# RetNet attention and MLP on one core: v's first chunks loaded as float32 by SyncE, and a reordered start

## The chip, the cores and the metric

The kernel runs on one core of one Trainium2 chip. The metric is the device time of one execution in microseconds. Before the change it is 302.19 us, the median of 3 runs (302.04 to 302.5).

## What is computed

The reference is a retention layer (attention with a decay mask instead of a softmax) followed by a two-layer MLP:

```python
B, H, S, D = 8, 8, 576, 64            # q, k, v: float32 [B, H, S, D]
scores = (1/sqrt(D)) * q @ k.transpose(0, 1, 3, 2)
gamma = 1 - 2.0 ** (-5 - arange(H))   # one decay for each head
Dmat = where(i >= j, gamma ** (i - j), 0)
ret = (scores * Dmat) @ v
x = ret.transpose(0, 2, 1, 3).reshape(B*S, H*D)   # 4608 x 512
h = x @ w_in                          # 512 x 2048
out = (h * sigmoid(1.702 * h)) @ w_out            # 2048 x 512, float32 out
```

## The kernel before

The decay gamma^(i-j) is split: v's rows are scaled by a factor of their position j (`vfac`, made from exponentials in `vraw`), and the result by a factor of i (`gq`). What is left of Dmat is a 0/1 mask. The sequence of a batch goes in chunks of 128 tokens (five, the last of 64); a running state (`psZ`, copied to `zq`) carries the earlier chunks. Batch 0 is done this way, chunk by chunk; batches 1 to 7 are done in wider steps woven into the matmuls of the MLP, which take nearly all of TensorE's time.

A recorder (`Rec.op`) notes every operation with the keys that it reads and writes, and derives the semaphore waits; each engine then runs its operations in the order in which they were noted. So the order of the calls in the code is the order of each engine's queue.

All loads go through GpSimd's queue (`load`, L216; the recorder's `POOL`) and are cast from float32 to bfloat16 on the way. A load of one chunk of q, k or v for all 8 heads has 1024 rows of 256 B. `load_w_in` (L240) and `load_w_out` (L245) load the MLP's weights on the same queue.

Batch 0's start, where the change lies, is a software pipeline over chunks n = 0 to 3:

- `transposes(n)` (L373): TensorE turns q and k of the chunk into one PSUM bank (`psT`, key "W").
- `evac_t(n)` (L379): ScalarE copies them to `qk`.
- `scores(n)` (L392) on TensorE into `psS`, then `mask_s(n)` (L402) on VectorE to `sm`; together `intra(n)`. There is one `psS`, so scores n+1 wait for mask n.
- `values(n)` (L415, L427, L442): TensorE's matmuls of `sm` and v, the state and the state's part; `evac_z` (L467) on ScalarE copies the state, `evac_o` (L480) on VectorE multiplies by `gq` and writes `xT`, the MLP's input.
- `scale_v(n)` (L358) multiplies a chunk of v by `vfac`; chunk 0's runs on VectorE, those of 1 to 3 on GpSimd between weight loads (chunk 3's into a second buffer `v3`, L362).
- `fill(count)` (L807): matmuls on zeros (`idle`) that keep TensorE busy where it would wait; they write `psH[0]`.

`constants_first` makes positions by two iotas on GpSimd (`posj`, `posa`), from them the identity, the mask and positions on VectorE (`rel`, `ident`, `mask`, `posi`), and on ScalarE eight exponentials for `vraw` (L273) and four for `gq`. `later_gq` (L327) makes the rest of `gq`. `constants_mask3` (L349) folds v's factor of chunk 3 into a mask.

After the four chunks, `hidden_split` (L712) begins the MLP with units f = 0 and 1, `hidden` (L695) goes on with f = 2 to 15 (f = 2, 3 use w_in's second load, f = 4 to 7 its third), and `project` (L746) multiplies by w_out. The third load of w_in covers columns of f = 4 to 7, the fourth those of f = 8 to 11.

The buffer `gT[1]` holds activations of the MLP's odd row blocks; at the start it is free, and `mask3` and `v3` lie in its rows 8 to 13.

## Time and profile before

| | |
|---|---|
| median of 3 runs | 302.19 us |
| the profiled execution | 302.22 us |
| its span, first to last instruction | 300.42 us |
| TensorE matmul busy | 292.5 us (97%) |
| VectorE busy | 122.3 us (41%) |
| ScalarE busy | 127.9 us (43%) |
| GpSimd busy | 154.8 us (52%) |
| DMA queue of GpSimd | 118384 packets, 18.36 MB |
| DMA queue of SyncE | 36432 packets, 16.92 MB |
| first w_in matmul starts at | 18.24 us |

The profile is one execution recorded by the hardware profiler; times in it count from the first instruction of the span, and 1.8 us of the execution lie outside it. Engines are named PE (TensorE matmul), PEld (its weight loads), DVE (VectorE), ACT (ScalarE), POOL (GpSimd) and SP (SyncE). A row names the engine, the line of the kernel, the operation and the tiles (out<-in).

### The profile page before, as it was taken

The page shows a single profiled execution, that of the slowest core. Times are in us where ns is not written, and L with a number is a line of the kernel's source. Part 1 is how long each engine was busy: PE and PEld are TensorE (multiplying, and loading weights), DVE is VectorE, ACT ScalarE, POOL GpSimd, SP SyncE. Part 2 cuts the span into 40 slices and gives each one's busy share as a digit, 9 for nine tenths or more (in the row PEclk, how much of TensorE's full clock was granted, in tenths as well). Part 3 has the DMA queues.
Part 4 walks back from the last instruction along what each step waited for, and adds up shares of the span by engine and source line. Part 5 has one row for each costly group of instructions (what it writes and reads, how often), then busy time and mean ns, then how long its engine had stood idle before and what let it go on. Part 6 is the DMA issues. An engine that isn't in the chain of part 4 may idle for free.

```text
span 300.4 us, 7696 instructions
## 1 busy us (share of the span) xinstructions
PE 292.5 (97%) x3395; PEld 148.9 (50%) x3395; DVE 122.3 (41%) x213; ACT 127.9 (43%) x215; POOL 154.8 (52%) x208
## 2 busy tenths in 40 slices
PE   7899999899999999999999999999999999999996
PEld 3454455757645444444444444544444444444444
DVE  6589735362525555334506143265236503000012
ACT  7676426614445503560375036602570266026600
POOL 8999679998967868677985796000000000000000
PEclk9999999999999999999999999999999999999999
DMA  9999999999999999999999999904720210020012
GB/s 69 145 183 207 177 171 161 193 129 138 178 143 163 163 117 191 173 136 142 135 213 138 127 186 155 85 1 101 173 41 2 105 37 2 0 107 35 0 57 85
DMA packets 154850, 35.78 MB, mean 119 GB/s; under 512 B 145472, under 2 KB 150336, under 8 KB 154816
## 3 DMA queue, kind: packets, MB, share of 16 engines
q0 software_dynamic: 118384, 18.36, 95.8%
q1 hardware_dynamic: 36432, 16.92, 31.6%
q8 instruction: 27, 0.44, 0.6%
q14 instruction: 7, 0.06, 0.1%
HBM read 36.70 MB, written 9.44 MB: 154 GB/s over the span
## 4 chain that ended last, share of the span: by engine, by line
PE 88%; POOL 4%; DMA 3%; ACT 2%; DVE 1%; issue 1%; POOLq 0%
PE psH L746 27%; PE psH L695 24%; PE psU L746 13%; PE psU L695 12%; DMA w_in_sb<-in_moe_w_in_dram 3%; PE psA L560 2%; PE psA L588 2%; PE psH L730 2%; PE psA L602 1%; PE psA L576 1%; POOL st_q L216 1%; PE psA L746 1%; POOL st_k L216 1%; PE psA L772 1%; POOL st_v L216 1%; ACT qk L379 1%
## 5 line engine op out<-in xcount | busy, mean ns | idle before, releaser
L746 PE MATMUL psH<-w_out_sb,gT 128*128 128x512 bf16 x368 | 87.0, 379 | 0.0
L695 PE MATMUL psH<-xT,w_in_sb 128*128 128x512 bf16 x332 | 79.2, 379 | 0.2 <-DMA w_in_sb<-in_moe_w_in_dram 0.2
L649 DVE TENSOR_TENSOR xT<-psA,gq 128x768 bf16<-128x768 f32 x21 | 20.1, 958 | 115.2 <-PE psA L576 115.2
L700 ACT ACTIVATE gT<-psH 128x512 bf16<-128x512 f32 x83 | 49.5, 597 | 26.0 <-PE psH L695 26.0
L229 POOL DMA_DIRECT2D st_k<-in_k_dram x70 | 53.0, 782 | 14.1 <-DMA st_k<-in_k_dram 13.1
L746 PEld LDWEIGHTS psH<-w_out_sb,gT 128*128 128x128 bf16 x368 | 35.0, 98 | 40.7 <-DVE sm L660 0.4
L229 POOL DMA_DIRECT2D st_v<-in_v_dram x70 | 52.0, 770 | 6.0 <-DMA st_v<-in_v_dram 4.0
L695 PEld LDWEIGHTS psH<-xT,w_in_sb 128*128 128x128 bf16 x332 | 32.1, 98 | 38.6 <-DMA w_in_sb<-in_moe_w_in_dram 0.7
L695 PE MATMUL psU<-xT,w_in_sb 128*128 128x512 bf16 x172 | 44.2, 379 | 0.1
L746 PE MATMUL psU<-w_out_sb,gT 128*128 128x512 bf16 x176 | 43.9, 379 | 0.0
L216 POOL DMA_DIRECT2D st_q<-in_q_dram x40 | 36.0, 899 | 9.7 <-DMA st_q<-in_q_dram 7.3
L755 ACT ACTIVATE osb<-psH 128x512 f32<-128x512 f32 x21 | 12.5, 597 | 57.6 <-PE psH L746 54.5
L700 ACT ACTIVATE gT<-psU 128x512 bf16<-128x512 f32 x43 | 25.7, 597 | 13.5 <-PE psU L695 13.5
L695 PEld LDWEIGHTS psU<-xT,w_in_sb 128*128 128x128 bf16 x172 | 16.5, 98 | 20.0 <-ACT gT L719 0.6
L746 PEld LDWEIGHTS psU<-w_out_sb,gT 128*128 128x128 bf16 x176 | 16.6, 98 | 19.4 <-issue 0.5
L358 DVE TENSOR_TENSOR st_v<-st_v,vfac 128x512 bf16<-128x512 bf16 x37 | 24.2, 683 | 0.9 <-DMA st_v<-in_v_dram 0.9
L676 DVE TENSOR_TENSOR zacc<-zacc,psA 128x256 f32<-128x256 f32 x49 | 20.5, 418 | 8.3 <-PE psA L588 7.1
L755 ACT ACTIVATE osb<-psU 128x512 f32<-128x512 f32 x10 | 6.0, 597 | 33.0 <-PE psU L746 33.0
L660 DVE TENSOR_TENSOR sm<-psA,maskw 128x768 bf16<-128x768 f32 x21 | 19.9, 948 | 0.0
L379 ACT ACTIVATE qk<-psA 128x1024 bf16<-128x1024 bf16 x10 | 10.2, 1022 | 10.5 <-PE psA L373 10.5
L758 DVE COPY osb<-psH 128x512 f32<-128x512 f32 x2 | 1.4, 692 | 26.9 <-PE psH L746 26.9
L560 PEld LDWEIGHTS psA<-sm,st_v 64*64 64x64 bf16 x504 | 7.5, 108 | 9.4 <-issue 8.7
(103 smaller groups left out, 231.0 us busy)
## 6 DMA issues: line engine op xcount, KB each, us to landing
out_dram<-osb SPq DMA_DIRECT2D x35, 256.0 KB, 4.0
st_q<-in_q_dram POOLq DMA_DIRECT2D x32, 128.0 KB, 7.2
st_k<-in_k_dram POOLq DMA_DIRECT2D x57, 64.0 KB, 7.5
st_v<-in_v_dram POOLq DMA_DIRECT2D x57, 64.0 KB, 7.3
w_out_sb<-in_moe_w_out_dram POOLq DMA_DIRECT2D x4, 512.0 KB, 11.8
w_in_sb<-in_moe_w_in_dram POOLq DMA_DIRECT2D x3, 512.0 KB, 8.9
st_k<-in_k_dram POOLq DMA_DIRECT2D x4, 128.0 KB, 4.5
st_v<-in_v_dram POOLq DMA_DIRECT2D x4, 128.0 KB, 4.6
```

The lines of the kernel that those rows point to most:

```text
L216: paced(R.op("POOL", lambda e, d=d, s=s: e.dma_start(d, s), w=[(nm, sl, c)], dma=(nm, sl, c), own=pace()))
L229: paced(R.op("POOL", lambda e: [e.dma_start(d, s) for d, s in parts], w=[(nm, sl, c)], dma=(nm, sl, c), parts=2, own=pace()))
L358: R.op(eng, lambda e: e.tensor_tensor(t, t, f, ALU.mult), r=[("vfac", min(b, 1))], w=[("v", sl, c)])
L379: R.op("ACT", lambda e: e.activation(qk[n % NQK].ap(), psT, AF.Copy), w=[("qk", n % NQK, 0), ("qk", n % NQK, 1)], ps=["W"])
L560: i = e.matmul(psA[half(t), 2 + u, at : at + 64], rows_of(st_v, m_out, g, u, 4 * u + 2 * t + j), smw[si(m_out)][half(r), j, 2 * blk + t, : ...
L649: R.op("DVE", lambda e: e.tensor_tensor(xT[:, :, t0 : t0 + 192].rearrange("p (u j) n -> p u j n", u=2), psA[:, 2:4, 0:384].rearrange("p u ...
L660: R.op("DVE", lambda e: e.tensor_tensor(o, i, k, ALU.mult), r=["maskw"], w=[("sm", si(m))], ps=["S"])
L676: R.op("DVE", lambda e, to=to, src=src, was=was: e.tensor_tensor(to, was, src, ALU.add), r=[("zacc", (blk - 1) % 3)], w=[("zacc", blk)], p ...
L695: i = e.matmul(bank, w_in_sb[:, a, 128 * f : 128 * f + 128], xT[:, a, 512 * c : 512 * c + 512], start=(a == 0), stop=(a == 3))
L700: R.op("ACT", lambda e: e.activation(gT[c % 2][:, f, :], bank, AF.Gelu_apprx_sigmoid), w=[("gT", c % 2, f)], ps=[key])
L746: i = e.matmul(bank, gT[c % 2][:, f, 128 * r : 128 * r + 128], w_out_sb[:, f, :], start=(f == 0), stop=(f == NF - 1))
L755: R.op("ACT", lambda e: e.activation(osb[m].ap(), bank, AF.Copy), w=[("osb", m)], ps=[key])
```

## The change

- `load_early(c)`: v's chunks 0 to 2 of batch 0 are loaded by SyncE as float32, without a cast, into rows 0 to 5 of `gT[1]` (two rows for each chunk), first of all. `scale_v` of these chunks reads the float32 copy and writes `st_v`.
- `scale_v(0)` and `scale_v(1)` are on VectorE ahead of the first `mask_s`; `scale_v(2)` is on GpSimd between the second and third load of w_in, `scale_v(3)` after the third.
- The first transposes alternate between two banks: chunks 1 and 3 go to `psH[0]` (`turned`), the fills to `psH[1]`.
- `transposes(1)` and `evac_t(1)` come ahead of `intra(0)`, and so on: each chunk's transposes one step earlier in TensorE's order. There are 13, 4, 3, 2 and 2 fills (24) in place of 14, 4, 3, 3 and 3 (27).
- One VectorE product (`posj` by `lnh`) and one exponential make `vraw`, in place of eight exponentials.
- The memsets (`constants_zero`) come first on VectorE; `mask` is made last of the first constants.
- GpSimd's order: q's chunk 0 ahead of the iotas, then k's chunk 0, q and k of chunks 1 to 3, w_in's first load, v's chunk 3, and the other weight loads.

```diff
@@ -158,6 +158,7 @@
         tiny = sb("tiny", [P, 1], FP32)
         idle = sb("idle", [P, 512], BF16)
         lng = sb("lng", [P, HP], FP32)
+        lnh = sb("lnh", [P, H], FP32)
         vraw = sb("vraw", [P, H, NC], FP32)
         vfac = [sb(f"vfac{i}", [P, H, NC], FP32) for i in range(2)]
         zacc = sb("zacc", [P, 3, 2 * 128], FP32)
@@ -250,35 +251,52 @@
             R.op("POOL", lambda e: e.iota(t.ap(), pattern, base=base, channel_multiplier=mul,
                                           allow_small_or_imprecise_dtypes=True), w=[name])
 
-        def constants_first():
-            iota(posj, "posj", [[128, NC]], 0, 1)
-            iota(posa, "posa", [[1, 128]], 0, 0)
-            R.op("DVE", lambda e: e.tensor_scalar(
-                rel.ap(), posa.ap(), posj[:, 0:1], None, ALU.subtract),
-                r=["posa", "posj"], w=["rel"])
+        def load_early(c):
+            s = v[0, :, 128 * c : 128 * c + 128, :].rearrange("h p d -> p h d")
+            d = early(c).rearrange("p (h d) -> p h d", d=DH)
+            R.op("SP", lambda e: e.dma_start(d, s), w=early_keys(c), dma=("early", c))
+
+        def early(c):
+            return gT[1][:, 2 * c : 2 * c + 2, :].rearrange("p f n -> p (f n)").bitcast(FP32)
+
+        def early_keys(c):
+            return [("gT", 1, 2 * c), ("gT", 1, 2 * c + 1)]
+
+        def constants_zero():
             R.op("DVE", lambda e: e.memset(idle.ap(), 0.0), w=["idle"])
+            for h in range(H):
+                R.op("DVE", lambda e, h=h: e.memset(lnh[:, h : h + 1], -math.log(gamma(h))),
+                     w=["lnh"])
             for hp in range(HP):
                 for hh in range(2):
                     R.op("DVE", lambda e, hp=hp, hh=hh: e.memset(
                         lng[64 * hh : 64 * hh + 64, hp : hp + 1],
                         math.log(gamma(2 * hp + hh))), w=[("lng", hp, hh)])
+
+        def constants_first():
+            iota(posj, "posj", [[128, NC]], 0, 1)
+            iota(posa, "posa", [[1, 128]], 0, 0)
+            R.op("DVE", lambda e: e.tensor_tensor(
+                vraw.ap(), posj.ap().unsqueeze(1).to_broadcast([P, H, NC]),
+                lnh.ap().unsqueeze(2).to_broadcast([P, H, NC]), ALU.mult),
+                r=["posj", "lnh"], w=["vraw"])
+            R.op("DVE", lambda e: e.tensor_scalar(
+                rel.ap(), posa.ap(), posj[:, 0:1], None, ALU.subtract),
+                r=["posa", "posj"], w=["rel"])
             R.op("DVE", lambda e: e.tensor_single_scalar(ident.ap(), rel.ap(), 0.0, ALU.is_equal),
                  r=["rel"], w=["ident"])
-            R.op("DVE", lambda e: e.tensor_single_scalar(mask.ap(), rel.ap(), 0.0, ALU.is_ge),
-                 r=["rel"], w=["mask"])
             for c in range(1, NC):
                 R.op("DVE", lambda e, c=c: e.tensor_single_scalar(
                     posi[:, c - 1, :], posa.ap(), 128.0 * c, ALU.add), r=["posa"], w=["posi"])
-            for h in range(H):
-                R.op("ACT", lambda e, h=h: e.activation(
-                    vraw[:, h, :], posj.ap(), AF.Exp, scale=-math.log(gamma(h))),
-                    r=["posj"], w=["vraw"])
+            R.op("ACT", lambda e: e.activation(vraw.ap(), vraw.ap(), AF.Exp), w=["vraw"])
             for hp in range(HP):
                 R.op("ACT", lambda e, hp=hp: e.activation(
                     gq[:, hp, 0:128], posa.ap(), AF.Exp, scale=lng[:, hp : hp + 1]),
                     r=["posa", ("lng", hp, 0), ("lng", hp, 1)], w=[("gq", 0)])
             R.op("DVE", lambda e: e.tensor_single_scalar(
                 vfac[0].ap(), vraw.ap(), float(QK_SCALE), ALU.mult), r=["vraw"], w=[("vfac", 0)])
+            R.op("DVE", lambda e: e.tensor_single_scalar(mask.ap(), rel.ap(), 0.0, ALU.is_ge),
+                 r=["rel"], w=["mask"])
 
         def constants_second():
             R.op("DVE", lambda e: e.memset(zs.ap(), 0.0), w=[("zs", 0), ("zs", 1)])
@@ -354,6 +372,11 @@
             sl = b % NST
             t = st_v[:, sl, c, :].rearrange("p (h d) -> p h d", d=DH)
             f = vfac[min(b, 1)][:, :, c : c + 1].to_broadcast([P, H, DH])
+            if n < 3:
+                i = early(n).rearrange("p (h d) -> p h d", d=DH)
+                R.op(eng, lambda e: e.tensor_tensor(t, i, f, ALU.mult),
+                     r=[("vfac", 0)] + early_keys(n), w=[("v", sl, c)])
+                return
             if to is None:
                 R.op(eng, lambda e: e.tensor_tensor(t, t, f, ALU.mult),
                      r=[("vfac", min(b, 1))], w=[("v", sl, c)])
@@ -366,18 +389,26 @@
             b, c = divmod(n, NC)
             return [(0, st_q, "q", b % NST, c), (1, st_k, "k", b % NST, c)]
 
+        def turned(n):
+            if n < NC - 1 and n % 2:
+                return psH[0].ap().bitcast(BF16).rearrange("p (a h n) -> p a h n", a=2, h=HP), ("H", 0)
+            return psT, "W"
+
         def transposes(n):
+            to, key = turned(n)
+
             def fn(e):
                 for a, t, nm, sl, c in sides(n):
                     for hp in range(HP):
-                        i = e.matmul(psT[:, a, hp, :], t[:, sl, c, 128 * hp : 128 * hp + 128],
+                        i = e.matmul(to[:, a, hp, :], t[:, sl, c, 128 * hp : 128 * hp + 128],
                                      ident.ap(), is_transpose=True)
                 return i
-            R.op("PE", fn, r=["ident"] + [(nm, sl, c) for a, t, nm, sl, c in sides(n)], ps=["W"])
+            R.op("PE", fn, r=["ident"] + [(nm, sl, c) for a, t, nm, sl, c in sides(n)], ps=[key])
 
         def evac_t(n):
-            R.op("ACT", lambda e: e.activation(qk[n % NQK].ap(), psT, AF.Copy),
-                 w=[("qk", n % NQK, 0), ("qk", n % NQK, 1)], ps=["W"])
+            to, key = turned(n)
+            R.op("ACT", lambda e: e.activation(qk[n % NQK].ap(), to, AF.Copy),
+                 w=[("qk", n % NQK, 0), ("qk", n % NQK, 1)], ps=[key])
 
         def half(r):
             return slice(64 * r, 64 * r + 64)
@@ -783,18 +814,19 @@
                     r=[("osb", m)], dma=("osb", m))
 
 
+        constants_zero()
+        for c in range(3):
+            load_early(c)
+        load(0, 0, "q")
         constants_first()
-        for c in range(3):
+        load(0, 0, "k")
+        for c in range(1, 4):
             load(0, c, "qk")
-        load(0, 0, "v")
-        load(0, 3, "qk")
-        for c in range(1, 4):
-            load(0, c, "v")
         load_w_in(0, 1)
+        load(0, 3, "v")
         load_w_in(1, 2)
+        scale_v(2, "POOL")
         load_w_in(2, 4)
-        scale_v(1, "POOL")
-        scale_v(2, "POOL")
         scale_v(3, "POOL", v3)
         load_w_in(4, 6)
         load_w_in(6, 8)
@@ -804,44 +836,45 @@
         def fill(count):
             def fn(e):
                 for _ in range(count):
-                    i = e.matmul(psH[0].ap(), idle[:, 0:128], idle.ap(), start=True, stop=True)
+                    i = e.matmul(psH[1].ap(), idle[:, 0:128], idle.ap(), start=True, stop=True)
                 return i
-            R.op("PE", fn, r=["idle"], ps=[("H", 0)])
+            R.op("PE", fn, r=["idle"], ps=[("H", 1)])
 
         def quarters(bank):
             return bank.ap().rearrange("p (h n) -> p h n", h=HP)
 
         third = [(psO, "O"), (quarters(psU), "U"), (quarters(psH[1]), ("H", 1))]
-        fill(14)
+        fill(13)
         transposes(0)
         later_gq(0)
         later_gq(1)
+        later_gq(2)
         evac_t(0)
         constants_second()
         constants_mask3()
-        later_gq(2)
+        scale_v(0)
+        scale_v(1)
         fill(4)
+        transposes(1)
+        later_gq(3)
+        evac_t(1)
         intra(0)
-        transposes(1)
-        evac_t(1)
-        later_gq(3)
         fill(3)
-        intra(1)
         transposes(2)
         evac_t(2)
-        scale_v(0)
-        fill(3)
-        intra(2)
+        intra(1)
+        values(0, third[0])
+        evac_z(0)
+        evac_o(0, third[0])
+        fill(2)
         transposes(3)
         evac_t(3)
-        values(0, third[0])
-        evac_o(0, third[0])
-        evac_z(0)
-        fill(3)
-        intra(3)
+        intra(2)
         values(1, third[1])
         evac_z(1)
         evac_o(1, third[1])
+        fill(2)
+        intra(3)
         values(2, third[0])
         evac_z(2)
         evac_o(2, third[0])
```

## Prediction

> **What bounds the kernel now.** I read first the page's engine table (TensorE 97% busy), then the chain of waits of the first 24 us, then the timeline of that stretch, then the DMA view of single windows. After 22.4 us TensorE loses only 1.6 us in five waits of at most 0.34 us (waits of PE, 22 us to the end: 0.7, 0.3, 0.2, 0.2, 0.2), so the change, which touches only the start, is worth what the start gains. The chain of waits in order of time (start us, us, what):

> ```profile
> 1.37 1.04 POOL st_q L216
> 2.42 0.89 POOL st_k L216
> 3.31 0.87 POOL st_q L216
> 4.18 0.88 POOL st_k L216
> ...
> 12.04 1.37 POOL w_in_sb L240 x2
> 13.41 8.94 DMA w_in_sb<-in_moe_w_in_dram
> ```

> GpSimd issues twelve q, k, v loads at 0.87 us each, then w_in; the third w_in load lands at 22.35 and releases TensorE. That chain is the last wait by a little only; a second chain runs beside it, in the timeline (start us, busy us, engine, line; idle time before in brackets):

> ```profile
> 8.84 0.40 PE L392 MATMUL psA<-qk 64*128 64x128 bf16 x8 [0.25 <-ACT qk L379]
> ...
> 11.00 0.40 PE L392 MATMUL psA<-qk 64*128 64x128 bf16 x8 [0.56 <-ACT qk L379]
> ...
> 13.15 0.40 PE L392 MATMUL psA<-qk 64*128 64x128 bf16 x8 [0.56 <-ACT qk L379]
> ...
> 17.31 0.41 PE L415 MATMUL psH<-sm,st_v 128*64 128x128 bf16 x8
> ...
> 18.24 0.82 PE L712 MATMUL psH<-xT,w_in_sb 128*128 128x384 bf16 x4
> ...
> 20.00 1.03 PE L695 MATMUL psH<-xT,w_in_sb 128*128 128x512 bf16 x4
> 21.12 1.04 PE L695 MATMUL psU<-xT,w_in_sb 128*128 128x512 bf16 x4
> 22.39 1.90 PE L695 MATMUL psH<-xT,w_in_sb 128*128 128x512 bf16 x8 [0.24 <-DMA w_in_sb<-in_moe_w_in_dram]
> ```

> Scores (L392) come every 2.16 us: scores, the next transposes behind them on TensorE, their 1.02 us copy on ScalarE, the next scores. The first w_in matmul starts at 18.24; I call this moment H. From H to unit f=4 it is 4.15 us. Unit f=3 starts at 21.12 and needs 4 x 0.216 = 0.86 us, so without the DMA wait f=4 would start at 21.98 = H + 3.74: w_in's lateness is worth 0.41 us, H itself everything else.

> Can DMA go faster than GpSimd issues? The DMA view of 6 to 13 us, and of 43.5 to 46.5 us, where loads stand in a queue:

> ```profile
> DMA packets 8287, 1.05 MB, mean 149 GB/s; under 512 B 8287, under 2 KB 8287, under 8 KB 8287
> ```
> ```profile
> DMA packets 3659, 0.46 MB, mean 152 GB/s; under 512 B 3659, under 2 KB 3659, under 8 KB 3659
> ```

> A load has 1024 rows of 256 B, so a load's packets take 7 / 8287 x 1024 = 0.865 us early (the issue rate) and 3 / 3659 x 1024 = 0.84 us with a queue. The engines are thus 97% full once the stream runs. What is empty is the time before 3.1 us (the first packet) and a dip near 4.5 to 5.2 us.

> **Part by part.** *v's chunks 0 to 2 on SyncE.* GpSimd loses three issues (2.6 us). The engines keep that work: 3 x 0.84 = 2.5 us. SyncE is free at about 0.75 us (its wait ends with 0.7); its queue's lag from issue to first packet is seen only for stores, 0.9 us (issue 235.10, then the GB/s row of the DMA view of 235 to 237, in 40 slices of 0.05 us: first bytes after 18 slices):

> ```profile
> GB/s 0 0 0 0 0 0 0 0 0 0 0 0 0 0 0 0 0 0 205 205 451 246 451 492 287 451 287 451 369 328 451 328 164 82 0 0 0 0 0 0
> ```

> So v's first packet is at 1.65, at the latest 2.4 (if this first load needs GpSimd's lag of 1.7 us). No load of SyncE's is in the trace: its cost lies between below nothing (it fills the empty start) and double (it writes 256 KB where the old one wrote 128 KB); I take the 0.84 us of the equal packets, the nearest row.

> *q's first load ahead of the iotas.* It issues at about 0.9 in place of 1.37. But the iotas and their 0.2 us gap now stand between it and k's first load, so k0 issues at 2.5 (before 2.42), q1 3.4, k1 4.3 (before 4.18); moved past v, q3 goes from 7.67 to 6.9 and k3 from 8.55 to 7.8. posj and posa come near 2.3 us instead of 1.17. The cover is VectorE's memsets: idle 0.27, lnh and lng 0.82 each, from 0.75 to 2.65; uncovered it would delay ident, due only at the first transposes (7 us), by some 0.5 us, which costs nothing.

> *One exponential.* Eight activations of 0.235 us (1.88) become one, about 0.25, behind one VectorE product. ScalarE then does gq by 4.9 and three later_gq of 0.72 by 7.2, before the first copy (7.76 before). This buys room and leaves the end untouched.

> *Order on TensorE and two banks.* Transposes 1 now stand ahead of scores 0, whose whole queue waits for k1. In before k1 landed at 4.18 + 4.4 = 8.55. After: the floor by issue is 4.3 + 4.4 = 8.7. By the engines: seven loads (three v, q0, k0, q1, k1) at 0.84 = 5.9, from 1.65 to 2.4 on, plus about 1.0 from last packet to landing: 8.5 to 9.3. I take 8.9, between. Then transposes 1, scores 0.46 later, first mask 0.44 after the scores start (9.28 - 8.84): 8.9 + 0.05 + 0.46 + 0.44 = 9.85, where before it was 9.28. That is a loss of 0.57.

> The gain: with evac_t(n+1) running during mask n, the cycle is VectorE's: mask 1.23, some 0.1 to TensorE, 0.44 to the next mask, 1.77; with evac_o (0.60 start to start) inside, 1.85. Three of them: 5.47, against 6.47 now (9.28 to 15.75); its worst end is 6.47, the best 5.3. q2, k2 land near 10.6 and q3, k3 near 12.3 by 0.84 each, in time. From the last mask to H: 1.23 + 0.1 + 0.93 (17.31 to 18.24) = 2.26; before 2.49, since values(2) lay between. H = 9.85 + 5.47 + 2.26 = 17.58, a gain of 0.66.

> *scale_v(0) and (1) on VectorE, (2) on GpSimd.* VectorE does them ahead of the first mask, behind mask3, from about 7.7: 2 x 0.68 = 1.4, to 9.1, if v1 is in by 8.4; v1 should land near 6 to 7.5. float32 in might cost up to the mask's 1.23 each: 10.2, 0.3 over. GpSimd's scale_v(2) (1.18) now stands before w_in's third load and scale_v(3), which waits for v3 (about 15.0), before the fourth: it ends at 16.2.

> *w_in.* Landings before: v3 16.0, then 17.84, 19.9, 22.35. After, eleven loads have landed by about 12.3, then by the same steps 14.2, v3 15.0, 17.1, 19.55. Unit f=4 wants it at 17.58 + 3.74 = 21.3: the 0.41 goes. The fourth lands at about 22.2, wanted at 24.8; batch 0's last chunk, 2.4 us earlier, keeps ahead too. The next limit is TensorE itself.

> Sum: 0.66 + 0.41 = 1.07 us off the profiled execution (302.22 us, span 300.42 and 1.8 around it). It lies 0.03 from the median, 302.19: 302.19 - 1.07 = 301.1.

> [...]

> **Rivals.** 1, *the SyncE loads fit the empty start*: k1 lands at the issue floor 8.7, the cycle at its best (5.3): H = 9.65 + 5.3 + 2.26 = 17.21, 1.03 + 0.41 off: 300.8. For it: nothing moves before 3.1 us now. Against: 2.5 us of work do not fit into 1.5 us.

> 2, *the wait moves to k1*: v takes its turn first, k1 lands at 9.3 and the cycle loses another 0.3 on VectorE: H = 18.3, only w_in's 0.41 is gained: 301.8, within 0.2% (0.6 us, what a measurement of this kernel tells from no change). For it: seven loads at a full rate. Against: the SyncE start, perhaps 1.65.

> 3, *slower: the engines are paid by bytes written*. At 149 GB/s a float32 load takes 262 KB / 149 = 1.76 us: seven loads take 3 x 1.76 + 4 x 0.84 = 8.6, from 2.1, plus 1.0: k1 at 11.7, 2.8 later than forecast, so H = 20.4 and 302.19 + 2.16 - 0.41 = 303.9. It decides from a k1 landing of 10.6 on (8.9 + 1.07 + 0.6). For it: 149 GB/s in every slice of the stage. Against: 201 GB/s written from 22 to 32 us with 1 KB pieces, and over 300 in the stores above. [...]

> 4, *the change doesn't shorten the cycle* (VectorE or the fills hold it at 2.16): H = 9.85 + 6.47 + 2.26 = 18.58, 302.1, within 0.2%.

> **Chances.** Forecast 0.45 (own range 300.7 to 301.5), rival 1 0.15, rival 2 0.15, rival 4 0.08, rival 3 0.12, and 0.05 for smaller slips past 302.8. Faster by over 0.2%: 0.45 + 0.15 = 0.60; within: 0.23; slower: 0.17. The range reaches from 300.4 (rival 1 less 0.4, the packets in the empty start costing nothing) through rivals 2 and 4 to 302.9 where slower begins, and leaves out most of rival 3.

> **What would show it.** Right: packets before 2.5 us; k1 landing at 8.7 to 9.3; masks 1.8 us apart; H at 17.3 to 17.9; no DMA wait before f=4. Wrong: transposes 1 waiting past 9.5, VectorE idle before scale_v, masks still 2.16 apart, or a new TensorE wait between 22 and 60 us that gives back the gain.

## The result, and the profile after

The changed kernel takes 305.56 us (median of 4 runs, 305.41 to 305.68) against 302.12 us (4 runs, 301.31 to 302.50): ratio 1.0116, 95% interval 1.0100 to 1.0132. The forecast was 301.1 us, with a range to 302.9. Measured again on two chips, the same kernel gave 304.39 (12 runs) and 303.81 (12 runs), ratios 1.0060 (1.0037 to 1.0082) and 1.0052 (1.0029 to 1.0076): slower each time, by an amount that differs. One run of the first of these and two of the second lie over 1.5% above the fastest; they are in the medians but not in the ratios, which are estimates of their own and not quotients of the medians.

The profiled execution took 305.63 us. From its page (engine table and slices):

```profile
span 303.8 us, 7689 instructions
PE 293.6 (97%) x3392; PEld 149.3 (49%) x3392; DVE 124.3 (41%) x223; ACT 126.7 (42%) x208; POOL 150.8 (50%) x204
```

The span grew by 3.4 us, TensorE's busy time by 1.1: it waits more, and some of its matmuls take longer. Its waits from 22 us to the end (engine, line, waited for: us in total, times, longest):

```profile
PE psA L607 <- issue: 1.7, 1, 1.7
PE psA L619 <- ACT qk L410: 0.7, 2, 0.3
PE psA L403 <- ACT qk L410: 0.6, 1, 0.6
```

The wait for w_in's third load is gone, as forecast; the first transposes of a later batch (L403) wait 0.6 us where they waited 0.3. New is 1.7 us, once, in the middle of a burst of small matmuls of the retention (L607), where TensorE waits for nothing that the profile shows.

The chain of waits at the start (start us, us, what):

```profile
1.24 1.03 POOL st_q L217
2.71 0.83 POOL st_k L217
3.54 0.92 POOL st_q L217
4.46 5.83 DMA st_k<-in_k_dram
```

and TensorE's timeline:

```profile
8.62 0.38 PE L403 MATMUL psA<-ident,st_q 128*128 128x128 bf16 x4 [1.86 <-DMA st_k<-in_k_dram]
...
10.42 0.38 PE L403 MATMUL psH<-ident,st_q 128*128 128x128 bf16 x4 [0.34 <-DMA st_k<-in_k_dram]
...
18.93 0.82 PE L743 MATMUL psH<-xT,w_in_sb 128*128 128x384 bf16 x4
...
22.68 1.67 PE L726 MATMUL psH<-xT,w_in_sb 128*128 128x512 bf16 x7
```

k's chunk 1 is issued at 4.46 and lands at 10.29. The first w_in matmul (H) starts at 18.93, not 17.58; unit f=4 follows 3.75 us later with no DMA wait, at 22.68 instead of 22.39.

**Where the 3.4 us arise.** Set the same activation of ScalarE in both traces side by side (the copies and activations of the MLP, one by one) and take the difference of their starts: +0.69 at the first unit, +0.28 from f=4 on (0.41 given back by w_in), +0.57 from 51.3 us (a copy to `osb` waits for an output store), **+3.75 from about 70 us**, +3.40 at the end. So the start costs 0.3, and 3.18 us arise between 66 and 71 us. There the chain of waits reads

```profile
65.93 0.03 PE psA L607 x4
65.96 1.67 issue
67.64 0.26 PE psA L607 x8
67.89 1.77 PE psH L777 x4
69.66 1.71 PE psU L777 x4
```

and the stage table (stretch, length, busy us and instructions of PE, PEld, DVE, ACT, POOL, then PEclk, DMA share, GB/s), first line after, second line before:

```profile
68.20:71.50 3.30, 3.30 (x10) 1.22 (x9) 1.90 (x3) 0.00 (x0) 2.99 (x5) 0.53 2.09 175
```
```profile
68.20:71.50 3.30, 3.30 (x23) 2.10 (x22) 0.00 (x0) 1.53 (x3) 2.53 (x5) 1.00 2.09 139
```

After the 1.67 us of idleness the granted clock is halved for one piece of 3.413 us (67.92 to 71.33 in the trace's clock records, 0.28 us behind the wait's end): four matmuls take 1.77 and 1.71 us instead of 0.86, and the five units from 67.89 to 74.00 take 6.11 us where they take 4.42 in before. So 1.43 us of added wait (before waits 0.24 at this place) and 1.69 of halved clock.

### The profile page after: what moved, and what is told of

It reads as the page before. It is cut to its first block, busy times and chain, and to the rows that moved or that the text cites. A ratio compares the mean times of both kernels' runs of the same rounds, so it can differ in the third digit from the quotient of the medians.

```text
span 303.8 us, 7689 instructions
## 1 busy us (share of the span) xinstructions
PE 293.6 (97%) x3392; PEld 149.3 (49%) x3392; DVE 124.3 (41%) x223; ACT 126.7 (42%) x208; POOL 150.8 (50%) x204
## 4 chain that ended last, share of the span: by engine, by line
PE 89%; DMA 3%; DVE 3%; ACT 2%; issue 1%; POOL 1%; POOLq 0%; ACTq 0%
PE psH L777 26%; PE psH L726 23%; PE psU L777 13%; PE psU L726 12%; PE psA L591 2%; PE psA L619 2%; DMA st_k<-in_k_dram 2%; PE psH L761 2%; PE psA L633 1%; PE psA L607 1%; PE psA L777 1%; DVE sm L433 1%; PE psA L803 1%; DMA out_dram<-osb 1%; ACT qk L410 1%
## 5 line engine op out<-in xcount | busy, mean ns | idle before, releaser
L777 PE MATMUL psU<-w_out_sb,gT 128*128 128x512 bf16 x176 | 44.6, 385 | 0.0
L381 DVE TENSOR_TENSOR st_v<-st_v,vfac 128x512 bf16<-128x512 bf16 x36 | 23.4, 680 | 0.0
L691 DVE TENSOR_TENSOR sm<-psA,maskw 128x768 bf16<-128x768 f32 x21 | 19.9, 947 | 0.0
L607 PE MATMUL psA<-qk,zw 64*64 64x64 bf16 x448 | 11.0, 193 | 1.7 <-issue 1.7
L410 ACT ACTIVATE qk<-psA 128x1024 bf16<-128x1024 bf16 x8 | 8.2, 1022 | 9.9 <-PE psA L403 9.9
## 6 DMA issues: line engine op xcount, KB each, us to landing
w_out_sb<-in_moe_w_out_dram POOLq DMA_DIRECT2D x4, 512.0 KB, 10.2
```

The costliest lines, as they stand in the source:

```text
L381: R.op(eng, lambda e: e.tensor_tensor(t, t, f, ALU.mult), r=[("vfac", min(b, 1))], w=[("v", sl, c)])
L410: R.op("ACT", lambda e: e.activation(qk[n % NQK].ap(), to, AF.Copy), w=[("qk", n % NQK, 0), ("qk", n % NQK, 1)], ps=[key])
L607: i = e.matmul(psA[half(t), 2 + u, at : at + 64], zw[half(j), g, 1 - u, t, :], q_of(m_out, g, j, u, t), start=False, stop=(par == 1), skip ...
L691: R.op("DVE", lambda e: e.tensor_tensor(o, i, k, ALU.mult), r=["maskw"], w=[("sm", si(m))], ps=["S"])
L777: i = e.matmul(bank, gT[c % 2][:, f, 128 * r : 128 * r + 128], w_out_sb[:, f, :], start=(f == 0), stop=(f == NF - 1))
```

## Experiments

Each run stands beside runs of the kernel before on the same chip. ("After" is the changed kernel.) Besides the medians I use each run's mean granted clock: 0.994 is one halved piece of 3.4 us in 300 (the profiled run of after), 0.989 is two (that of after again, below), 1.000 is none. Where an early text names a theory by a letter, three were in play: SyncE's loads at the start are the cause; the place of TensorE's instructions in the program is (a late fetch of them); or the moment is, at which later work meets the stream of loads.

**1. The new order without SyncE's loads** (after; v's chunks 0 to 2 loaded by GpSimd as before, and their `scale_v` back where they were in before: chunk 0's on VectorE behind the second mask, those of 1 and 2 on GpSimd).

```diff
-        for c in range(3):
-            load_early(c)
...
+        load(0, 0, "v")
+        load(0, 3, "qk")
+        for c in range(1, 4):
+            load(0, c, "v")
```

> The changed kernel with v's chunks 0 to 2 loaded by GpSimd as bfloat16 again, at their old places among the q and k loads; two banks, new order, one exponential and q first stay. Theory A (SyncE's loads crowd out q0, k0, k1 at the start; the late loss of 3.1 us is the alignment of TensorE's instruction fetch at about 65 us with the DMA traffic, which any shift can move): k1 lands at 8.7 to 8.9 in place of 10.3, first w_in matmul at 17.4 to 17.8, and the late stall of 1.67 us with the half clock need not be there; time near 302 (301.3 to 302.6), or near 305 if the stall falls in by chance. Rival B (the new order waits for k1 whatever loads v): k1 at 9.5 or later and first w_in matmul at 18.5 or later; time 304 or more.

304.56 us against 302.34, ratio 1.0075 (1.0051 to 1.0100). Timeline of TensorE:

```profile
9.02 0.38 PE L403 MATMUL psH<-ident,st_q 128*128 128x128 bf16 x4 [1.10 <-DMA st_k<-in_k_dram]
...
13.65 0.41 PE L446 MATMUL psA<-sm,st_v 128*64 128x128 bf16 x8 [1.92 <-DVE st_v L381]
...
19.73 0.82 PE L743 MATMUL psH<-xT,w_in_sb 128*128 128x384 bf16 x4
```

Without the three loads k1 is there 1.4 us earlier (transposes 1 at 9.02, not 10.42; it lands at 8.89). Yet H comes later still, at 19.73, where 17.4 to 17.8 was expected: values(0) waits 1.92 us, with transposes 3 queued behind. That wait isn't for v's load, which is issued at 7.07 and lands 4.4 us later, at 11.49; `scale_v(0)` stands behind the second mask in VectorE's order and starts as soon as that one ends:

```profile
11.77 1.22 DVE L433 TENSOR_TENSOR sm<-psA,mask 128x1024 bf16<-128x1024 f32 x1 [0.54 <-PE psA L423]
12.91 0.68 DVE L381 TENSOR_TENSOR st_v<-st_v,vfac 128x512 bf16<-128x512 bf16 x1
```

So this run shows what SyncE's three loads do to k1. What the new order would be worth without them it doesn't show, because `scale_v(0)` stands in the way here. 4 of its 10 runs have a halved piece of the clock.

**2. SyncE's loads without the new order** (before, with `load_early` of v's chunks 0 to 2 and their `scale_v` reading it).

```diff
+        for c in range(3):
+            load_early(c)
...
-        load(0, 0, "v")
...
-        for c in range(1, 4):
-            load(0, c, "v")
+        load(0, 3, "v")
```

> The kernel before with one part of the change: SyncE loads v's chunks 0 to 2 as float32 first of all, GpSimd has three loads fewer; order, banks, exponentials as before. Theory A: q0 and k0 are crowded out (k0 lands near 8.5 instead of 6.7, k1 near 10), the first scores come at 10.5 instead of 8.84 and the cycle stays 2.16, so the first w_in matmul comes at 19.5 to 20; f=4 follows 3.75 later, 1.0 to 1.4 later than before: 303.1 to 303.6, and more only if the late stall falls in. Rival B (the loads of SyncE cost little by themselves): first w_in matmul at 18.6 or earlier, 301.8 to 302.3.

305.12 against 302.34, ratio 1.0088 (1.0058 to 1.0118).

```profile
10.61 0.40 PE L408 MATMUL psA<-qk 64*128 64x128 bf16 x8 [0.25 <-ACT qk L395]
...
12.76 0.40 PE L408 MATMUL psA<-qk 64*128 64x128 bf16 x8 [0.56 <-ACT qk L395]
...
19.99 0.82 PE L728 MATMUL psH<-xT,w_in_sb 128*128 128x384 bf16 x4
```

Scores 0 start at 10.61 instead of 8.84 and keep the old step of 2.15 us; H is 1.75 us late. The loads alone put the first transposes, which wait for k0, at 8.88 instead of 7.12, 1.8 us later; the reorder then wins back about 1.1 of it (H at 18.93 against 19.99). H came where it was expected (19.5 to 20), the time did not (303.1 to 303.6): a wait of 0.92 us in the burst near 67 us is part of the rest.

**3. SyncE's loads of v each behind k of its chunk** (after; the load waits until k has landed; `scale_v` later to match).

```diff
-            R.op("SP", lambda e: e.dma_start(d, s), w=early_keys(c), dma=("early", c))
+            R.op("SP", lambda e: e.dma_start(d, s), r=[("k", 0, c)], w=early_keys(c),
+                 dma=("early", c))
```

> The changed kernel with SyncE's three loads each waiting for the k of their chunk to land (scale_v(0) behind the first mask, scale_v(1) and (2) on GpSimd behind w_in's third load). Theory A (the loads at the very start crowd out q0, k0, k1): k1 lands near 9.0 again, the first scores come at 9.5 and the first w_in matmul at 17.5 to 18.2 in place of 18.93; f=4 at 21.3 to 22.0; the time is then 301.4 to 302.2 plus what the fetch waits take (0 to 3). Rival B (the new order itself waits): first w_in matmul at 18.9 or later.

312.69 against 302.12, ratio 1.0344 (1.0325 to 1.0364). k0 and k1 are early (transposes at 7.03 and 8.94), but v arrives far too late: GpSimd's `scale_v` waits 5.46 and 4.17 us for its two chunks, and TensorE's clock is halved from 17.72 to 27.96. The DMA view from 19 to 20 us, while the third v load is awaited (queue: packets, MB, share):

```profile
q0 software_dynamic: 158, 0.14, 86.3%
q1 hardware_dynamic: 163, 0.04, 31.4%
```

In this window the two queues move nearly the same number of packets, 158 and 163, while GpSimd's (w_in) hold 0.9 KB on average and SyncE's 0.25 KB. At that count a load of 1024 packets takes about 6.3 us, an estimate (1024 / 163), and v's was slow indeed: SyncE has issued the third by 12.61, and `scale_v` waits for it until 22.66, 10 us later; in after the median from issue to landing of these three loads is 3.9 us.

**4. Only one load on SyncE** (after; v0 on SyncE, v1 behind k2 and v2 behind k3 on GpSimd, `scale_v(1)` behind the second mask, w_in's third load ahead of `scale_v(2)`, and 15 and 5 fills in place of 13 and 4).

```diff
-        for c in range(3):
-            load_early(c)
+        load_early(0)
...
+        load(0, 1, "qk")
+        load(0, 2, "qk")
+        load(0, 1, "v")
+        load(0, 3, "qk")
+        load(0, 2, "v")
...
-        fill(13)
+        fill(15)
...
-        scale_v(1)
-        fill(4)
+        fill(5)
```

> The changed kernel with only v's chunk 0 on SyncE; chunks 1 and 2 are loaded by GpSimd behind k2 and k3, scale_v(1) runs on VectorE behind the second mask, w_in's third load stands ahead of scale_v(2); 15 and 5 first fills in place of 13 and 4, so that TensorE's instructions stand at the places of the kernel before. Theory A (crowding at the start grows with what SyncE loads first): k1 lands at 9.0 to 9.4 in place of 10.3, the first w_in matmul comes at 17.6 to 18.2, f=4 at 21.4 to 22.0 against 22.39 in the kernel before; with fetch waits like those of the kernel before 301.4 to 302, at worst 303. Rival B (the order waits for k1 as in the changed kernel): first w_in matmul at 18.8 or later, 302.5 or more.

302.80 against 302.38, ratio 1.0023 (1.0001 to 1.0045); after on the same chip has 1.0060 (1.0037 to 1.0082).

```profile
8.65 0.38 PE L403 MATMUL psH<-ident,st_q 128*128 128x128 bf16 x4
...
10.71 0.38 PE L403 MATMUL psA<-ident,st_q 128*128 128x128 bf16 x4 [0.37 <-DMA st_k<-in_k_dram]
...
13.33 0.38 PE L403 MATMUL psH<-ident,st_q 128*128 128x128 bf16 x4 [0.68 <-DMA st_k<-in_k_dram]
...
18.49 0.82 PE L743 MATMUL psH<-xT,w_in_sb 128*128 128x384 bf16 x4
```

k1 is no longer late (8.65), f=4 starts 0.16 us earlier than in before, there is no wait in the burst at 65 us, and this profiled execution took 301.8 us, 0.42 less than the one of before. The median doesn't show that gain: 301.4 to 302 was expected. This is the best of the versions in that direction, and it isn't faster than before. The first transposes start at 7.02 without a wait, so fewer loads and more fills act together here: 2 of its 12 runs have a halved piece, and which of the two keeps it away the run can't tell.

**5. Is it the moment?** One VectorE memset of about 0.5 us is put ahead of `evac_o(2)`, in before and in after:

```diff
+        for _ in range(1):
+            R.op("DVE", lambda e: e.memset(osb[2].ap(), 0.0), w=[("osb", 2)])
```

> The kernel before with one memset of an output buffer (about 0.5 us) on VectorE ahead of evac_o(2), which delays the first w_in matmul by some 0.5 us and touches nothing else. Theory A (alignment): a shift of the start by this much changes the stalls at 50 to 75 us by more than the shift: either by over 1 us with a drop of the clock, or by nothing; the time is then not 302.2 + 0.1 to 0.5 but can be 304 to 306. Rival C (the late loss belongs to the changed parts, not to the shift): 302.3 to 302.7, no stall over 0.4 us between 60 and 70 us, clock 0.999.

> The changed kernel with one memset of about 0.5 us on VectorE ahead of evac_o(2), which delays the first w_in matmul by some 0.45 us (from 18.9 to 19.4). Theory A (from 60 us on TensorE waits for 16 KB fetches of its own instructions, delayed by DMA traffic; each wait ends about 1.2 to 1.5 us after the end of a fetch): the stall near 66 us changes its length, any stall of over 0.3 us ends 1.2 to 1.5 us after a fetch's end, time between 303 and 306.5, not simply 0.45 more. Rival C (the stall of 1.67 us belongs to that burst): the same stall, 0.45 us more than the changed kernel on the same chip (e5's 305.8 and 305.6 before: about 306).

Before so shifted: 302.66 against 302.34, ratio 1.0003 (0.9984 to 1.0021), and 0.56 us of wait in the burst (0.24 without). After so shifted: 304.74 against 302.12, 1.0083 (1.0056 to 1.0109), wait 1.40 us, and 8 of its 10 runs have a halved piece. A shift of half a microsecond alone is not what costs microseconds.

**6. Is it the place in the program?** The fills ahead of the first transposes are made narrower and twice as many, in after (26 of 256 columns) and in before (28); or changed in number, 16 in after and 11 in before:

```diff
-        fill(13)
+        fill(26, 256)
```

> The changed kernel with its first 13 fills (512 columns) made 26 of 256 columns: the same TensorE time, 26 instructions more ahead of everything. Theory A (the stall of 1.67 us is TensorE waiting for its own instructions): every later 16 KB fetch falls 26 instructions earlier in the program, the stall at the L607 matmuls near 66 us moves or goes, the clock holds: 302.3 to 302.8, or another value if a fetch meets the traffic elsewhere. Rival C (the stall is fixed to that burst by its data or buffers): the same 1.67 us at the same matmuls, 305.5.

> The kernel before with its first 14 fills (512 columns) made 28 of 256 columns: the same TensorE time at the start, 28 more instructions ahead of everything, nothing else changed. Theory A: the first w_in matmul stays at 18.2 to 18.3, but the fetches fall 28 instructions earlier in the program, so stalls appear at other places (near 66, 100 or 111 us as in e5) or the 0.24 us one goes: 302 to 304.5 with the start unchanged. Rival C (the late loss belongs to the changed parts): no stall over 0.4 us, 302.0 to 302.5.

> The changed kernel with 16 first fills in place of 13: TensorE waits for k0 until 8.6 us anyway, so the start keeps its time, and the program's instructions stand at the same places of the fetches as in the kernel before. If the place in the program decides (theory A1): the stall near 66 us falls back to 0.2 to 0.5 us, 302.3 to 303. If the moment against the DMA traffic decides (theory A2): the stall stays over 1 us, 304 to 306. Rival C: the same 1.67 us.

> The kernel before with 11 first fills in place of 14 (TensorE then idles up to 1.4 us before the first transposes): TensorE's later instructions stand 6 places earlier, as in the changed kernel; nothing else changes, and no data comes later. Theory A1 (the place of the 16 KB fetches in the program decides): the first w_in matmul stays at 18.2 to 18.4, the stall near 66 us grows from 0.24 to over 0.8 us: 303 to 305. Theory A2 (the moment against the DMA traffic decides): 302.0 to 302.6. Rival C (the late loss belongs to the changed parts): 302.0 to 302.4 with the stall at 0.2 to 0.3 us.

After with 26 narrow fills: 305.76, ratio 1.0104 (1.0055 to 1.0153), waits 0.82 us at 66 and 0.98 at 111 us. Before with 28: 302.36, 1.0017 (0.9988 to 1.0045), no clear change; its profiled run has no wait in the burst, but one of 1.34 us behind ScalarE at 100 us. Before with 11, which moves TensorE's instructions forward as the change does: 302.07, 0.9988 (0.9969 to 1.0007), and the wait in the burst stays 0.25 us:

```profile
65.48 0.26 PE L576 MATMUL psA<-qk,zw 64*64 64x64 bf16 x9 [0.25 <-issue]
```

So the place alone doesn't bring the loss. Yet after with 16 fills gave 303.18, 1.0048 (1.0024 to 1.0073), with a wait of 0.77 us, between what the two theories had forecast, and 9 of its 10 runs have a clock of 0.999 or 1.000. Three fills that end before k0 has landed cost nothing; what do they change? They shorten TensorE's wait for k0, from 1.86 to 1.27 us in the profiled runs.

**7. After once more, and the wait for k0 shortened by fills.** First the changed kernel itself, again:

> The changed kernel itself, on the chip of the other two. Theory A: the start as in its first profile (k1 at 10.3, first w_in matmul at 18.9); the stall near 66 us 0.8 to 1.7 us with or without the drop of the clock from run to run, so 304 to 306 with some spread.

304.39, and 10 of 12 runs have a clock of 0.994 or less; the profiled one is the longest of the twelve, 308.02 us, with two halved pieces (9.34 to 12.75 us, behind a wait of 2.30 us for k0, and 70.78 to 74.19 us), the second behind this:

```profile
69.79 0.26 PE L607 MATMUL psA<-qk,zw 64*64 64x64 bf16 x8 [2.25 <-issue]
```

Then three kernels together on another chip: the 24 fills handed out otherwise, 17, 3, 2, 1, 1 in place of 13, 4, 3, 2, 2, so that all that stands behind the last fill keeps its place; 20 fills ahead of the first transposes; and after itself.

```diff
-        fill(13)
+        fill(20)
```

> After with its 24 fills handed out as 17, 3, 2, 1, 1 in place of 13, 4, 3, 2, 2: everything behind the last fill keeps its place in TensorE's program, only the wait for k's chunk 0 (1.86 us in after) is covered by about 0.9 us more. If the halved clock after an idle window of TensorE is most of what after loses beside the late k1: at least two thirds of the runs have a mean clock of 0.998 or more (after itself: 2 of 12), median 302.9 to 303.4, as with 16 fills (303.18). If the place of TensorE's instructions decides (the fetch of them), nothing changes against after: most runs at 0.994, median 304.2 to 304.8.

> After with 20 fills in place of 13 ahead of the first transposes: the wait for k's chunk 0 is all but gone (k0 lands near 8.6, the fills end near 8.5); everything behind stands 7 matmuls further on in TensorE's program. If idle windows halve the clock: clock 0.998 or more in at least 9 of 12 runs, median 302.8 to 303.3; the start is no earlier than in after (first w_in matmul at 18.9 to 19.1), so it stays slower than before by 0.5 to 0.9. If the place in the program decides, the outcome is open between 302.5 and 305.5 and not ordered by the clock.

> After itself beside the two others on the same chip: most runs at a mean clock of 0.994 or less, median 304.2 to 305.6. Where its profile has a clock of 0.994, the half-clock piece of 3.4 us lies either near 9 to 13 us (behind the wait for k0) or near 68 to 74 us (behind the wait in the burst of small matmuls).

| kernel | fills ahead of the first transposes | runs with a clock below 0.998 | median us (before) | ratio, 95% interval |
|---|---|---|---|---|
| after, three measurements | 13 | 20 of 28 | 305.56, 304.39, 303.81 | 1.0116, 1.0060, 1.0052 (above) |
| after, 16 fills | 16 | 1 of 10 | 303.18 (302.12) | 1.0048 (1.0024 to 1.0073) |
| after, fills moved | 17 | 1 of 12 | 303.06 (302.01) | 1.0027 (1.0011 to 1.0043) |
| after, 20 fills | 20 | 0 of 12 | 302.78 (302.01) | 1.0023 (1.0007 to 1.0039) |
| before, four chips | 14 | 0 of 103 | 302.34, 302.12, 302.38, 302.01 | |

The last two kernels and after's third measurement ran side by side on one chip: a clock below 0.998 in 6 of 12 runs with 13 fills, in 1 of 12 with 17, in none of 12 with 20. (For after itself more than half of the runs and 304.2 us or more were expected; it gave 6 and 303.81.) The moved fills keep all later places and change the idle time, and the halved clock is nearly gone. With 20 fills there is no wait in the burst above 0.2 us either, and the offset against before hardly changes, from +0.35 at 56 us to +0.28 at the end:

```profile
65.86 0.30 PE L607 MATMUL psA<-qk,zw 64*64 64x64 bf16 x12
66.33 0.81 PE L777 MATMUL psH<-w_out_sb,gT 128*128 128x512 bf16 x3 [0.16 <-issue]
```

The wait for k0 was expected to be all but gone with 20 fills. In the profiled run it is 1.30 us: the clock rose at 4.60 us there, and at 6.48 in after's, so 20 fills took 6.16 us where 13 had taken 5.57.

Among the runs of after in its second and third measurement, the 8 at full clock have a median of 303.17, the 13 with one halved piece 304.33: about 1.2 us goes with the halved piece and the wait ahead of it, and 0.8 to 1.2 remains against before. The late start is +0.3 of that in the profiles (after with 20 fills: +0.28 at the end, while its median lies 0.77 above before's); the rest isn't explained. The one run of the moved fills with a halved clock is the profiled one, 304.49 us: there k0 came late (transposes 0 at 9.36, a wait of 2.71 us), and the clock was halved behind it, 0.51 from 11.4 to 14.8 us.

**The wait in the burst.** The page of before, like that of after, shows 27 packets of instructions, 0.44 MB, so 16 KB each, on a DMA queue of their own:

```profile
q8 instruction: 27, 0.44, 0.6%
```

I call the packet ahead of the burst the fetch. In the traces with a wait below, the wait ends 1.2 to 1.6 us after the fetch has landed. Take the fetch against TensorE's own work (its start or landing, less the offset of the run's activations between 56 and 64 us, less the 62.96 or 64.13 of before):

| profiled run | fetch starts late by, us | it lands late by, us | wait in the burst, us |
|---|---|---|---|
| one SyncE load | -0.8 | -0.8 | 0 |
| after, 20 fills | -0.3 | 0.0 | under 0.2 |
| before | 0 | 0 | 0.24 |
| v on GpSimd | -0.3 | 0.2 | 0.47 |
| before, 11 fills | 0.1 | 0.2 | 0.25 |
| after, fills moved | 0.4 | 0.4 | 0.53 |
| before, shifted | 0.2 | 0.5 | 0.56 |
| SyncE loads alone | 0.5 | 0.7 | 0.92 |
| after, 16 fills | 0.5 | 0.7 | 0.77 |
| after, third time | 0.6 | 0.8 | 1.03 |
| v behind k | 0.7 | 0.9 | 1.35 |
| after, shifted | 1.1 | 1.3 | 1.40 |
| after | 1.4 | 1.4 | 1.67 |
| after again | 1.8 | 2.0 | 2.25 |

The wait grows as the fetch lands later, about microsecond for microsecond. (The two kernels with narrow fills aren't in the table; their burst stands at another place of the program.) From this I infer that TensorE waits there for its own instructions; no view names it. What makes the fetch late isn't settled: neither the place in the program (before with 11 fills) nor a plain delay (before shifted) did it. The DMA engines are loaded around it; in after the packet starts at 64.95, and SyncE's transposing DMAs follow (DMA view, 64 to 69 us in 40 slices):

```profile
GB/s 162 93 143 160 155 158 154 268 130 151 144 154 186 203 185 182 111 46 9 8 9 9 10 16 142 153 139 146 150 157 147 148 152 157 139 152 154 157 175 204
```

A hollow like that of 8 to 16 GB/s lies in before too (10 to 20 GB/s from 64.6 to 65.2 us), behind its own fetch, so it isn't the cause by itself. A kernel with the transposing DMAs moved wasn't tried.

## Why the prediction was wrong

**The step that failed first: when k1 lands.** Forecast were a first packet at about 2.0, seven loads at 0.84 = 5.9, and 1.0 to landing: 8.9. Measured: first packet 1.86, seven loads 6.97 us (the last of GpSimd's first 4096 packets, four loads, starts at 8.83), 1.46 to landing: 10.29. Two terms are mis-sized: the seven loads by 1.1 us, the landing by 0.5. The larger is the price of the float32 loads. While SyncE's queue ran almost alone (2 to 4 us: 1887 of its packets, 9 of GpSimd's), its first two loads took 1.24 and 1.13 us for 1024 packets each, not the 0.84 of the equal packets. GpSimd's first packet then came at 3.92 instead of 3.12 in before (2.68 us behind its issue, not 1.75; with one SyncE load, in the fourth experiment, it came at 2.98), and GpSimd's first load took 2.17 us beside SyncE's third, where in before it took 1.25. The DMA view of 4 to 6.5 us, after and then before:

```profile
q0 software_dynamic: 1317, 0.17, 103.8%
q1 hardware_dynamic: 1091, 0.27, 64.4%
```
```profile
q0 software_dynamic: 2285, 0.29, 180.9%
```

2408 packets against 2285: the engines carry hardly more, and GpSimd's queue, which everything waits for, loses 968 of them, nearly a whole load. The early start took in 1948 of SyncE's 3072 packets before 4 us; the others, over a third, didn't fit. (SyncE's lag from issue to first packet was 1.12 us; the store's row that the prediction read gives 0.8, not 0.9.) Rival 3 had the right direction and its own price too high (1.76 us a load; measured 1.13 to 1.24), and k1 stayed below the 10.6 us from which it was to decide the sign.

**The other steps of the start held.** From k1 to the first mask 1.11 (forecast 0.95); three masks 11.40 to 16.73 = 5.33 (5.47), so the new order with two banks did shorten the cycle from 2.16 to 1.78 and rival 4 is out; last mask to H 2.20 (2.26). Late by 1.39 + 0.16 - 0.14 - 0.06 = 1.35, H became 18.93. With f=4 at H + 3.75 (3.74) and w_in's 0.41 gone, this start is worth 0.69 - 0.41 = +0.28 us: 302.19 + 0.28 = 302.5, inside the forecast range but late by what k1 lost. `scale_v` on VectorE ran from 7.00 to 8.28 and was in nobody's way; the one exponential and q's earlier load (issued at 1.24, not 0.9) changed nothing that the path shows.

**The step that decided it: "the change, which touches only the start, is worth what the start gains".** That sentence failed. The profiled execution loses 0.28 at the start, 0.29 at an output store, 1.43 in TensorE's wait in the burst and 1.69 by the halved clock, 50 us later, and gets 0.35 back by the end: of the 3.18 that the offsets show at 66 to 71 us these two make 3.12, and 0.28 + 0.29 + 3.18 - 0.35 is the 3.40 at the end. The prediction named "a new TensorE wait between 22 and 60 us" as a sign of being wrong (it came at 66); the fills went uncosted: the change was described with 24 in place of 27 of them, but nothing said that 13 would now stand before a wait of 1.86 us instead of 14 before none. That a halved clock could cost anything was no rival at all. The experiments tie it to TensorE's idle time: with the same loads and order and 16 to 20 fills ahead of the first transposes, 2 of 34 runs have it; with 13, 20 of 28 (on one chip, 1 of 24 against 6 of 12). In the first profiled run it came behind the wait in the burst, not behind the one for k0; how the fills at the start shorten that later wait isn't shown.

**What stays open:** what makes the fetch at 65 us late in after, and why more fills at the start make it earlier; why the three measurements of the changed kernel differ by 1.7 us, while those of before differ by 0.4; and the part of the remaining 0.8 to 1.2 us that the late start doesn't explain.

## What to carry to other kernels

Here the second queue's loads at the start were paid for by the first queue: from 4 to 6.5 us, 968 packets of GpSimd's for 1091 of SyncE's. Move only what is due before the critical load, and price it by the packets that the critical queue loses, not by the issue time that its engine saves. Where a change makes TensorE wait longer, fill that wait again: here seven more idle matmuls, which left the first transposes where they were (8.65 us, in after 8.62), took back 1.0 us of the median and narrowed the runs from 302.13 to 307.50 us to 301.95 to 303.55. And read the mean clock of every run, not only of the profiled one: here runs at 0.994 and 1.000 by turns were the sign of waits behind which the clock is halved in some runs and not in others.

## What the hardware showed that was not expected

  | profiled run | piece, us | TensorE idle in it, us | next piece |
  |---|---|---|---|
  | after again | 5.92 to 9.34 | 2.30 | halved |
  | v behind k | 14.31 to 17.72 | 2.27 | halved |
  | after again | 67.36 to 70.78 | 2.24 | halved |
  | after, fills moved | 7.91 to 11.32 | 1.99 | halved |
  | after, shifted | 6.37 to 9.78 | 1.97 | halved |
  | after, narrow fills | 4.18 to 7.60 | 1.95 | full |
  | SyncE loads alone | 5.19 to 8.60 | 1.94 | full |
  | after | 6.48 to 9.89 | 1.86 | full |
  | v behind k | 10.89 to 14.31 | 1.77 | full |
  | after | 64.50 to 67.92 | 1.75 | halved |
  | v on GpSimd | 12.19 to 15.60 | 1.72 | full |

  In this table the two groups part between 1.95 and 1.97 of 3.41 us; the wait of 3.02 us fell into two pieces, 1.95 and 1.07. The one exception is after's piece with the burst, part of whose busy time is matmuls of 64x64. This is read from the traces; no run varied the idle time alone, and the ends of matmuls are modelled.
- TensorE stood still inside a burst of matmuls for up to 2.25 us (after again) with nothing in the profile to wait for, and the wait ended 1.2 to 1.6 us after a 16 KB packet of instructions had landed. That it waits for its own instructions is my inference from the table above.
- Two busy queues moved nearly equal numbers of packets, 163 and 158 from 19 to 20 us of the third experiment, though one moved 0.04 MB with them and the other 0.14.
